# Three-stage attention and expert kernel on one core: border columns copied by the engines that make the parts, padding cleared ahead, low parts of the weights on VectorE, and the work between two stages laid out anew

## The chip, the core and the metric

One core of a Trainium2 chip. The metric is the device time of one execution in microseconds; three runs of the kernel before gave 1315.1 us in the median (1314.43 to 1315.68). The engines are named as in the profile: PE is TensorE's matmul, PEld its weight load, DVE VectorE, ACT ScalarE, POOL GpSimd, SP SyncE, which issues nearly all DMAs.

## What is computed

For 8 batches of 576 positions, 8 heads of 64:

```python
kv  = einsum('bhsd,bhse->bhde', k, v)
x   = einsum('bhsd,bhde->bhse', q, kv); x = x / sqrt(mean(x*x) + 1e-6) * g_norm   # 4608 x 512
h   = relu(x @ w_in)                                   # 512 -> 1024
y   = (h * sigmoid(conv3(h, conv_w))) @ w_out          # conv3: three taps along the positions, zero padding
out = y + relu(layernorm(y) * g_ln @ w_ch1) @ w_ch2    # 512 -> 2048 -> 512
```

## The kernel before

**Number format.** Each fp32 operand of the large products is a high part, rounded to TensorE's fp32r format by a copy, and a low part (value less high part); a product is three passes, high x high, high x low, low x high. High parts are copies on ACT, low parts subtractions on DVE or POOL. Three weight matrices arrive as 8-byte numbers and are first converted (`cv_act` on ACT, `cv_vec` on DVE, `cv_pool` on POOL, L245 to L269).

**Stage A**, the first 535 us. The 4608 positions are 36 tiles of 128 (t), three to a chunk (c = 0 to 11). A tile is made by `qkv` (PE), `st_a`, `st_v`, `st_p`, `x_norm` (ACT, DVE, POOL, DVE), `tx_first` (PE transpose), then `xe_a` (L479, ACT, high part) and `xe_l` (L502, DVE, low part) into the chunk's two tiles x_t[c]. These are 386 or 388 columns wide: 384 positions and border columns, which belong to the neighbouring chunk or are zero at the edges of a group of three chunks. `new_xt` (L457) allocates them and clears the zero columns on POOL; `xe_h` (L512) copies the border columns on POOL, two copies for each part, when the first tile of a chunk is there. So the first product of a chunk that is not the last of its group waits for the first tile of the next chunk and for `xe_h`. For each i (8 slices of 128 hidden columns in each of 12 chunks): `gemm1` (L534, 12 matmuls), `conv_a`, `conv_t`, `conv_v` (ACT, ACT, DVE twice, L582), `gate_a`, `gate_v` (ACT, DVE L599), `gsplit_a`, `gsplit_l` (ACT, DVE or POOL, L608), `gemm2` (L610, 9 matmuls). The last `gemm2` of a chunk is followed by `y_evac` and `y_store`.

**Stage B**, from 535 us. Six chunks of 768 positions. `ln_stat`, `ln_p`, `ln_a` normalise a tile (DVE L716 to L719, POOL, ACT); for chunk 0 it is turned by PE (`tz_first`, `tz_evac`), for the others by 16 stream transposes on DVE (`tz`, L750, through `blocks`, L470). The first product uses seven matrix products in place of eight: `z_sum` (L753, four DVE subtractions) and `z_hi`, `z_lo` (L766, L771) make seven factors. A chunk has 8 blocks (p). In a block PE runs p1, p2, p6, p5, p7, p4, p3 (L783, six matmuls each) and, between them, 12 `part`s of the block before (L861, three matmuls each). They share two PSUM banks for the first product: p1 of the next block waits until `r_lo` "21" (L843, DVE) has read the bank that p4 ended, p2 of the next until `c_add` "12" (L831, DVE) has read that of p3.

**Weights of stage B.** w_ch1 is split during stage A: `w1_sum`, `w1_hi` (ACT), `w1_lo` (L677, POOL, 32 subtractions: 24 of 128x512, 8 of 128x256), `w1_store` to DRAM. w_ch2 is converted and split (16 slices, `split_w1` on POOL, L289) during the blocks of chunk 0, two slices to a block, and stored for the later chunks.

**Order.** Every step has a slot, a number; the program is all steps in order of slot, and each engine takes its instructions in that order. `at(slot, fn, ...)` sets it; for slots before 25 two lists of names (`ORDERS`) replace it. gemm1 of slice i stands at slot 2i, its chain one to three slots later, its gemm2 at 2i + 7; so slot 160 is the first gemm1 of chunk 10. END_A = 192 is the slot of p1 of the first block, a block has 14 slots. Lines L981 to L1118 place the steps that the change moves. Buffers come from rotating pools; `xt` holds six tiles, for x_t, and later for z's inputs and sums.

Of the kernel before, what the change touches and what calls it, by code (L numbers as in the profile page):

```python
# [10 lines left out]
F32 = mybir.dt.float32  # L11
# [1162 lines left out]
```

## Time and profile before

| | |
|---|---|
| median of three runs | 1315.1 us (1314.43 to 1315.68) |
| the profiled execution | 1316.47 us |
| its span in the trace | 1314.7 us |
| busy in the span: PE, PEld, DVE | 1270.2, 1135.6, 902.5 us |
| ACT, POOL | 550.8, 277.7 us |
| mean granted clock of TensorE | 0.984 |

The profiled execution lies 1.4 us above the median; 1.8 us of it lie outside the span. A row of the timeline is a start, a duration, engine, line, operation, what it writes and reads, how many alike follow each other, and in brackets how long the engine was idle before and what ended that. A row of the windows gives the busy time of each engine in a stretch, TensorE's granted clock (1.00 is 2.4 GHz, 0.50 is 1.2 GHz), the busy share of the DMA engines and their GB/s.

### The profile page before, as it was taken

To read this page: it belongs to the slowest core of one execution; us is meant where nothing else is said; L and a number is where in the kernel's file an instruction comes from. 1 tells how busy PE (TensorE), PEld (TensorE's weight loads), DVE (VectorE), ACT (ScalarE), POOL (GpSimd) and SP (SyncE) were. 2 spreads that over 40 slices of the span, in tenths; PEclk is the share of its full clock that TensorE was granted. 3 is DMA by queue.
4 is the path that set the end of the run, shared out by engine and by line. 5 is a ranking of instruction groups with operands and counts; after the bars stand their busy time and mean duration, and the time that the engine had idled before them with its cause. 6 is when DMAs were issued, how large, how long until landed. Compare 5 with 4: busy or idle time off the path is not lost.

```text
span 1314.7 us, 19363 instructions
## 1 busy us (share of the span) xinstructions
PE 1270.2 (97%) x6949; PEld 1135.6 (86%) x6949; DVE 902.5 (69%) x1755; ACT 550.8 (42%) x1067; POOL 277.7 (21%) x296
## 2 busy tenths in 40 slices
PE   6789999999999999899999999999999999999998
PEld 5678898989888899788889898999999899998997
DVE  4898887878888877777766666667666766663223
ACT  3664565655665566544342223223322322232221
POOL 3473543332333321233310100000000001000000
PEclk9789999999999999999999999999999999999999
DMA  9455366345643223477668674865676576656561
GB/s 299 110 158 141 104 185 160 110 143 149 171 119 100 86 96 113 153 256 256 248 248 298 206 233 157 307 193 192 229 251 202 183 286 222 206 206 256 176 224 49
DMA packets 184052, 245.90 MB, mean 187 GB/s; under 512 B 92668, under 2 KB 121364, under 8 KB 183956
## 3 DMA queue, kind: packets, MB, share of 16 engines
q1 hardware_dynamic: 182032, 243.59, 57.6%
q10 hardware_dynamic: 1924, 1.07, 0.3%
q8 instruction: 55, 0.90, 0.3%
q14 instruction: 41, 0.34, 0.1%
HBM read 202.66 MB, written 41.94 MB: 186 GB/s over the span
## 4 chain that ended last, share of the span: by engine, by line
PE 60%; DVE 19%; ACT 8%; SPq 5%; DMA 4%; issue 3%; POOL 1%; DVEq 0%; ACTq 0%; POOLq 0%
PE accB L861 27%; PE u L783 14%; PE v L783 7%; DVE a L582 6%; PE c L783 4%; PE accA L617 4%; SPq L391 4%; PE h L542 3%; DVE a L599 2%; DVE zx L475 2%; ACT a L558 1%; ACT g L603 1%; ACT a L593 1%; DVE g L608 1%; ACT hs L567 1%
## 5 line engine op out<-in xcount | busy, mean ns | idle before, releaser
L861 PE MATMUL accB<-w2s,r 128*128 128x512 f32 x1440 | 376.1, 393 | 0.0
L861 PEld LDWEIGHTS accB<-w2s,r 128*128 128x128 f32 x1440 | 267.3, 188 | 38.5
L783 PE MATMUL u<-z,w1s 128*128 128x384 f32 x1152 | 235.4, 339 | 8.3 <-DVE r L843 5.7
L542 PE MATMUL h<-xt,win 128*128 128x386 f32 (+1 forms) x1152 | 226.6, 346 | 6.3 <-POOL xt L519 6.2
L783 PEld LDWEIGHTS u<-z,w1s 128*128 128x128 f32 x1152 | 207.0, 188 | 27.6 <-DVE r L843 8.6
L617 PE MATMUL accA<-wout,g 128*128 128x512 f32 x864 | 223.9, 404 | 2.2 <-DVE ya L627 1.2
L542 PEld LDWEIGHTS h<-xt,win 128*128 128x128 f32 x1152 | 206.4, 192 | 14.8 <-POOL xt L519 8.5
L617 PEld LDWEIGHTS accA<-wout,g 128*128 128x128 f32 x864 | 160.9, 191 | 34.4 <-DVE ya L627 2.1
L838 ACT ACTIVATE r<-t 128x384 fp32r<-128x384 f32 x144 | 75.7, 526 | 262.5 <-DVE t L831 262.5
L825 ACT COPY u<-u 128x384 f32<-128x384 f32 x144 | 68.7, 477 | 217.8 <-PE u L783 217.8
L582 DVE SCALAR_TENSOR_TENSOR a<-hs,cols,a 128x384 f32<-128x384 f32 x192 | 137.2, 714 | 29.5 <-ACT a L558 25.5
L475 DVE STREAM_TRANSPOSE zx<-xc 32x128 f32<-32x128 f32 x480 | 145.2, 303 | 7.5
L843 DVE SCALAR_TENSOR_TENSOR r<-t,r 128x384 fp32r<-128x384 f32 x144 | 80.4, 558 | 85.3 <-ACT r L838 85.3
L726 POOL TENSOR_SCALAR mv<-mv 128x1 f32<-128x1 f32 x36 | 25.0, 694 | 478.8 <-DVE mv L717 470.9
L783 PE MATMUL v<-z,w1s 128*128 128x384 f32 x576 | 116.9, 337 | 0.0
L783 PEld LDWEIGHTS v<-z,w1s 128*128 128x128 f32 x576 | 103.7, 188 | 8.2
L831 DVE TENSOR_TENSOR t<-v,u 128x384 f32<-128x384 f32 x96 | 53.4, 556 | 73.7 <-ACT u L825 55.4
L593 ACT ACTIVATE a<-a 128x384 f32<-128x384 f32 x96 | 50.4, 525 | 114.3 <-DVE a L582 114.2
L447 POOL TENSOR_TENSOR r<-ss,mhalf 128x8 f32<-128x8 f32 x36 | 66.8, 1856 | 77.5 <-DVE ss L442 75.2
L861 PE MATMUL accB<-w,r 128*128 128x512 f32 x288 | 77.7, 402 | 0.0
L268 POOL TENSOR_TENSOR cvw<-cvw,rnw 128x512 int32<-128x512 int32 x32 | 43.3, 1353 | 160.5 <-DVE cvw L261 108.2
L599 DVE TENSOR_TENSOR a<-hs,a 128x384 f32<-128x384 f32 x96 | 62.9, 655 | 19.1 <-ACT a L593 18.9
(106 smaller groups left out, 1380.3 us busy)
## 6 DMA issues: line engine op xcount, KB each, us to landing
w1s<-w_d SPq DMA_DIRECT2D x144, 512.0 KB, 5.5
w2s<-w_d SPq DMA_DIRECT2D x80, 512.0 KB, 5.2
raw_w<-in_moe_w_ch SPq DMA_DIRECT2D x32, 512.0 KB, 5.6
w_d<-w1f SPq DMA_DIRECT2D x24, 512.0 KB, 2.8
w1s<-w_d SPq DMA_DIRECT2D x48, 256.0 KB, 5.4
y_dr<-ya SPq DMA_DIRECT2D x36, 256.0 KB, 2.3
yb<-y_dr SPq DMA_DIRECT2D x36, 256.0 KB, 5.4
yr<-y_dr SPq DMA_DIRECT2D x36, 256.0 KB, 6.1
```

Source lines behind the costliest of these rows:

```text
L447: nc.gpsimd.tensor_tensor(out=r, in0=x_r[t], in1=mhalf, op=ALU.pow)
L475: nc.vector.transpose(out=out[32 * i : 32 * i + 32, :, a : a + 32], in_=src[a : a + 32, :, i, :])
L542: nc.tensor.matmul(ps[:, 0:n], lhsT=w[:, a, kk, :], rhs=x_t[c][b][:, kk, 0:n], start=(m == 0), stop=(m == 3 * KD - 1),)
L582: nc.vector.scalar_tensor_tensor(out=av, in0=segs(c, h, j), scalar=cols[:, j * FA + f : j * FA + f + 1], in1=av, op0=ALU.mult, op1=ALU.add,)
L593: nc.scalar.activation(out=a, in_=a, func=ACTF.Sigmoid)
L599: nc.vector.tensor_tensor(out=av, in0=segs(c, h, 1), in1=av, op=ALU.mult)
L617: nc.tensor.matmul(acc[c][r], lhsT=g[:, a, r * P : (r + 1) * P], rhs=w[:, b, :], start=(f == 0 and n == 0), stop=(f == FA - 1 and n == len ...
L783: nc.tensor.matmul(ps[:, 0:HT], lhsT=w[:, a, kk, :], rhs=z[b][:, kk, :], start=(start and n == 0), stop=(n == 5), skip_group_check=True,)
L825: nc.scalar.copy(out=t, in_=ch[c, p, "u"][:, 0:HT])
L838: nc.scalar.activation(out=g[:, HI, :], in_=cu[c, p, h], func=ACTF.Relu)
L843: engine.scalar_tensor_tensor(out=g[:, LO, :], in0=cu.pop((c, p, h)), scalar=0.0, in1=g[:, HI, :].bitcast(F32), op0=ALU.max, op1=ALU.subtract)
L861: nc.tensor.matmul(ch[c][r], lhsT=g[:, a, rr * P : (rr + 1) * P], rhs=w[:, b, :], start=(p == 0 and n < RB and m == 0), stop=(p == NPB - 1 ...
```

## The change

1. **Border columns.** `xe_h` is gone. `border` copies the columns of the high part on ACT at the end of `xe_a`, those of the low part on DVE at the end of `xe_l`.
2. **Padding.** `new_xt` is a step of its own: chunks 0 to 2 at the very start, the others some slots ahead of their first `xe_a` (chunk 11 just ahead).
3. **w_ch1's low parts** (`w1_lo`) move from POOL to DVE, in the same slots.
4. **w_ch2's conversion and split** get new slots within the block, and `split_w1` moves from POOL to DVE.
5. **Chunk 0 of stage B**: `ln_stat` and what follows move from slots 160 to 180 to slots 148 to 168, `z_sum` from 186 to 178 and 180.4 (two halves), `z_hi` and `z_lo` from 187 to 194 to 179 to 193.
6. **Later chunks of stage B**: `z_sum` in two halves, the transposes `tz` in two halves of 8, other slots for the seven factors.
7. **End of stage A**: the last `gemm2` is issued tile by tile between p7, p4, p3 and p1, with one `y_evac` behind each.
8. `kv_pair` of batches 3 to 7: the four steps follow each other; the two lists for slots before 25 have a new order (only a few lines are shown).

```diff
--- before.py
+++ after.py
@@ ORDERS, second list
...
-        round_w0_win3 xe_h_3 xe_h_0 xe_h_1 gemm1_0 load_q2_3 cv_vec_win3 round_w0_win4 round_w0_wout0 consts3 conv_a_0
-        cv_pool_win3 consts4 load_w_wout7 kv_pair_1_0 kv_pair_1_1 cv_vec_win4 cv_pool_win4 load_w_wout4 load_w_wout5 consts5
...
+        round_w0_win3 load_q2_3 cv_vec_win3 round_w0_win4 round_w0_wout0 gemm1_0 conv_a_0 cv_pool_win3 consts3
+        consts4 cv_vec_win4 consts5 cv_pool_win4 kv_pair_1_0 load_w_wout4 kv_pair_1_1 load_w_wout7 kv_pair_1_2 load_w_wout5
...
@@ -454,6 +454,7 @@
             in1=x_r.pop(t).rearrange("p (h o) -> p h o", o=1).to_broadcast([P, H, D]),
             op=ALU.mult,
         )
+
     def new_xt(c):
         x_t[c] = [xt_p.tile([P, KD, XW], F32R, tag="xt", name=f"xt{c}_{a}") for a in range(2)]
         o, n = ((0, 1), (CH // 2 + 1, 2), (CH + 1, 1))[c % 3]
@@ -467,19 +468,26 @@
             nc.tensor.transpose(ps[:, j * P : (j + 1) * P], src[:, j * P : (j + 1) * P], ident)
         tp_ps[t] = ps.rearrange("p (k s) -> p k s", k=KD)
 
-    def blocks(out, src):
+    def blocks(out, src, rows=range(0, P, 32)):
 
         src = src.rearrange("p (k i j) -> p k i j", k=KD, i=P // 32)
-        for a in range(0, P, 32):
+        for a in rows:
             for i in range(P // 32):
                 nc.vector.transpose(out=out[32 * i : 32 * i + 32, :, a : a + 32], in_=src[a : a + 32, :, i, :])
 
     xe = {}
 
+    def border(t, a, copy):
+
+        c, r = divmod(t, TPC)
+        if r == 0 and c % 3 != 0:
+            here, prev = x_t[c][a], x_t[c - 1][a]
+            last = CH + 3 if (c - 1) % 3 == 1 else CH + 1
+            copy(out=prev[:, :, last : last + 1], in_=here[:, :, 1:2].bitcast(F32))
+            copy(out=here[:, :, 0:1], in_=prev[:, :, last - 1 : last].bitcast(F32))
+
     def xe_a(t):
         c, r = divmod(t, TPC)
-        if r == 0:
-            new_xt(c)
         xt = x_t[c]
         xf = tp_ps.pop(t)
         half = CH // 2
@@ -497,6 +505,7 @@
         for o, n, col in pieces:
             hi = xt[HI][:, :, col : col + n]
             nc.scalar.copy(out=hi, in_=xf[:, :, o : o + n])
+        border(t, HI, nc.scalar.copy)
         xe[t] = pieces, xf
 
     def xe_l(t, engine):
@@ -508,16 +517,7 @@
             engine.tensor_tensor(
                 out=xt[LO][:, :, col : col + n], in0=xf[:, :, o : o + n], in1=hi.bitcast(F32), op=ALU.subtract
             )
-
-    def xe_h(t):
-        c, r = divmod(t, TPC)
-        xt = x_t[c]
-        if r == 0 and c % 3 != 0:
-            prev = x_t[c - 1]
-            last = CH + 3 if (c - 1) % 3 == 1 else CH + 1
-            for a in range(2):
-                nc.gpsimd.tensor_copy(out=prev[a][:, :, last : last + 1], in_=xt[a][:, :, 1:2].bitcast(F32))
-                nc.gpsimd.tensor_copy(out=xt[a][:, :, 0:1], in_=prev[a][:, :, last - 1 : last].bitcast(F32))
+        border(t, LO, engine.tensor_copy)
 
 
     h_ps = {}
@@ -607,12 +607,12 @@
         a, g = a_sb.pop(i), g_sb[i]
         engine.tensor_tensor(out=g[:, LO, :], in0=a, in1=g[:, HI, :].bitcast(F32), op=ALU.subtract)
 
-    def gemm2(c, f):
+    def gemm2(c, f, tiles=range(TPC)):
         if f == 0:
             acc[c] = [ps_acc.tile([P, 512], F32, tag="acc", name=f"accA{c}_{r}") for r in range(TPC)]
-        g = g_sb.pop(c * FA + f)
+        g = g_sb[c * FA + f]
         w = wt["wout", f]
-        for r in range(TPC):
+        for r in tiles:
             for n, (a, b) in enumerate(PASSES):
                 nc.tensor.matmul(
                     acc[c][r],
@@ -650,6 +650,7 @@
     z_p = {}
     z_t = {}
     z_f = {}
+    z_more = {}
     w_f = {}
     w_t = {}
     ch = {}
@@ -747,8 +748,12 @@
     def tz_evac(c, r):
         nc.scalar.copy(out=new_z(c, r), in_=z_p.pop((c, r)))
 
-    def tz(c, r):
-        blocks(new_z(c, r), xc.pop((c, r)))
+    z_part = {}
+
+    def tz(c, r, i):
+        if i == 0:
+            z_part[c, r] = new_z(c, r), xc.pop((c, r))
+        blocks(*z_part[c, r], range(64 * i, 64 * i + 64, 32))
 
     def z_sum(c):
 
@@ -759,9 +764,16 @@
         sub = nc.vector.tensor_tensor
         sub(out=t12[:, 0], in0=b12, in1=b11, op=ALU.subtract)
         sub(out=t12[:, 1], in0=b22, in1=t12[:, 0], op=ALU.subtract)
-        sub(out=t34[:, 0], in0=b22, in1=b12, op=ALU.subtract)
-        sub(out=t34[:, 1], in0=b21, in1=t12[:, 1], op=ALU.subtract)
         z_t[c] = [b11, b21, t12[:, 1], t12[:, 0], t34[:, 0], b22, t34[:, 1]]
+
+        def rest():
+            sub(out=t34[:, 0], in0=b22, in1=b12, op=ALU.subtract)
+            sub(out=t34[:, 1], in0=b21, in1=t12[:, 1], op=ALU.subtract)
+
+        z_more[c] = rest
+
+    def z_sum2(c):
+        z_more.pop(c)()
 
     def z_hi(c, m):
         z = [big.tile([P, 2, HT], F32R, tag="big", name=f"z{c}_{m}_{a}") for a in range(2)]
@@ -971,8 +983,9 @@
     def h_xe(t):
         head(xe_a, t)
         head(xe_l, t, nc.vector)
-        head(xe_h, t)
-
+
+    for c in range(3):
+        at(START - 0.97, new_xt, c)
     h_q(0)
     h_q(1)
     head(x_norm, 0)
@@ -999,8 +1012,8 @@
 
     for c in range(NC):
         for r in range(TPC):
-            at(SA * c + SA - 2 + LAG + (1 if c < NC - 1 else 5), y_evac, c, r, nc.vector if r == 1 else nc.scalar)
-        at(SA * c + SA - 2 + LAG + (2 if c < NC - 1 else 6), y_store, c)
+            at(SA * c + SA - 2 + LAG + (1 if c < NC - 1 else 5.5 + 2 * r), y_evac, c, r, nc.vector if r == 1 else nc.scalar)
+        at(SA * c + SA - 2 + LAG + (2 if c < NC - 1 else 9.6), y_store, c)
     for t in range(len(HEAD), NT):
         s = tau(t)
         _, o_st, o_nm, _, o_xe = steps(t)
@@ -1008,9 +1021,10 @@
         for fn in (st_a, st_v, st_p):
             at(s + o_st, fn, t)
         at(s + o_nm, x_norm, t)
+        if t >= 3 * TPC and t % TPC == 0:
+            at(s + (o_st if t // TPC < NC - 1 else o_xe), new_xt, t // TPC)
         at(s + o_xe, xe_a, t)
         at(s + o_xe, xe_l, t, nc.vector)
-        at(s + o_xe, xe_h, t)
     for b in range(1, B):
         at(tau(kv_tile[b]) - 1, kv_evac, b)
 
@@ -1049,14 +1063,22 @@
         at(s + 4, w1_sum, p)
         for j in range(4):
             at(s + 5 + 2 * j, w1_hi, p, j)
-            at(s + 5 + 2 * j, w1_lo, p, j, nc.gpsimd)
+            at(s + 5 + 2 * j, w1_lo, p, j, nc.vector)
             at(s + 6 + 2 * j, w1_store, p, j)
     for f in range(FB):
-        s = END_A - 4 + 7 * f
-        at(s - 5, load_w, ("w2", f), src_out(w2, f))
-        rnd(s, ("w2", f))
-        spl(s + 3, ("w2", f), nc.gpsimd)
-        at(s + 4, w2_store, f)
+        p, i = divmod(f, 2)
+        s = END_A + SP * p
+        key = ("w2", f)
+        at(s - 9 + 6 * i, load_w, key, src_out(w2, f))
+        for fn, o in (
+            (round_w0, (-2, 3)[i]),
+            (cv_vec, (2.8, 10.7)[i]),
+            (cv_pool, (2.9, 10.8)[i]),
+            (split_w0, (8.6, 12.6)[i]),
+        ):
+            at(s + o, fn, key)
+        at(s + (10.65, 13)[i], split_w1, key, nc.vector)
+        at(s + (11, 14)[i], w2_store, f)
 
     for c in range(CB):
         for p in range(NPB):
@@ -1067,7 +1089,7 @@
                     at(s + 0.2, w2_load, c, 2 * p + i)
         for r in range(RB):
             if c == 0:
-                s = 160 + 4 * r
+                s = 148 + 4 * r
                 at(s - 6, y_load, c, r, "b")
                 at(s, ln_stat, c, r)
                 at(s, ln_p, c, r)
@@ -1080,11 +1102,14 @@
                 at(s, ln_stat, c, r)
                 at(s, ln_p, c, r)
                 at(s + 3, ln_a, c, r)
-                at(s + 4, tz, c, r)
-        at(END_A - 6 if c == 0 else base(c - 1, 7) - 3, z_sum, c)
+                at(s + 4, tz, c, r, 0)
+                at(s + 12.65, tz, c, r, 1)
+        s = END_A - 14 if c == 0 else base(c - 1, 7) + 0.9
+        at(s, z_sum, c)
+        at(s + (2.4 if c == 0 else 12.4), z_sum2, c)
         order = (M_A11, M_A12, M_S2, M_S1, M_S3, M_A22, M_S4)
         for n, m in enumerate(order):
-            s = END_A + (-5, -4, -3, -2, -1, 1, 2)[n] if c == 0 else base(c - 1, 7) + 2 * n + 1
+            s = END_A + (-13, -11, -9, -7, -5, -2, 1)[n] if c == 0 else base(c - 1, 7) + (1, 3, 5, 8, 14.9, 17.3, 19.3)[n]
             at(s + 0.1, z_hi, c, m)
             at(s + 0.2, z_lo, c, m, nc.vector)
         for r in range(RB):
@@ -1122,10 +1147,14 @@
         c, f = divmod(i, FA)
         at(2 * i, gemm1, i)
         s = 2 * i + LAG
-        at(s if s < END_A else END_A + 2 * (s - END_A) - 1, gemm2, c, f)
+        if i < FA * NC - 1:
+            at(s if s < END_A else END_A + 2 * (s - END_A) - 1, gemm2, c, f)
+        else:
+            for r in range(TPC):
+                at(END_A + 9 + 2 * r, gemm2, c, f, (r,))
     for b in range(1, B):
         for j in range(NP):
-            at(tau(kv_tile[b]) - 5 + j, kv_pair, b, j)
+            at(tau(kv_tile[b]) - (3 if b > 2 else 5 - j), kv_pair, b, j)
     for t in range(len(HEAD), NT):
         s = tau(t)
         at(s + steps(t)[0], qkv, t)
```

## Rows read from the trace of the kernel before

**Rows 1.** The page, first two lines: span, and what TensorE (PE) was busy.
```profile
span 1314.7 us, 19363 instructions
...
PE 1270.2 (97%) x6949; PEld 1135.6 (86%) x6949; DVE 902.5 (69%) x1755; ACT 550.8 (42%) x1067; POOL 277.7 (21%) x296
```

**Rows 2.** Windows: us of busy time by engine and (instructions), PEclk, DMA share, GB/s.
```profile
0.00:100.00 100.00, 74.57 (x512) 66.54 (x513) 73.34 (x121) 55.81 (x106) 55.02 (x60) 0.86 0.70 187
100.00:427.00 327.00, 324.37 (x2128) 288.02 (x2127) 264.88 (x450) 187.28 (x374) 117.87 (x118) 1.00 0.50 139
427.00:460.00 33.00, 31.42 (x166) 28.01 (x164) 28.09 (x48) 19.63 (x40) 11.38 (x11) 1.00 0.24 86
460.00:535.00 75.00, 74.40 (x382) 67.75 (x383) 58.98 (x101) 46.72 (x91) 13.91 (x18) 0.98 0.26 92
535.00:670.00 135.00, 124.43 (x584) 108.27 (x584) 100.48 (x214) 62.64 (x120) 46.18 (x43) 0.96 0.67 237
670.00:1314.70 644.70, 641.05 (x3183) 576.98 (x3181) 376.69 (x825) 178.68 (x340) 33.32 (x49) 1.00 0.64 217
```

**Rows 3.** Timeline, TensorE, 320 to 680 us: matmuls after an idle time, in brackets.
```profile
337.41 2.20 PE L542 MATMUL h<-xt,win 128*128 128x388 f32 x11 [0.36 <-POOL xt L519]
...
459.14 0.45 PE L542 MATMUL h<-xt,win 128*128 128x388 f32 x1 [1.16 <-POOL xt L519]
...
460.60 3.55 PE L542 MATMUL h<-xt,win 128*128 128x388 f32 x11 [1.02 <-POOL xt L519]
...
540.73 1.33 PE L783 MATMUL u<-z,w1s 128*128 128x384 f32 x6 [2.52 <-ACT u L825]
...
554.96 1.66 PE L783 MATMUL u<-z,w1s 128*128 128x384 f32 x6 [2.53 <-DVE r L843]
...
572.91 1.32 PE L783 MATMUL u<-z,w1s 128*128 128x384 f32 x6 [0.43 <-DVE r L843]
...
589.97 1.31 PE L783 MATMUL u<-z,w1s 128*128 128x384 f32 x6 [1.10 <-DVE r L843]
...
660.35 1.31 PE L783 MATMUL c<-z,w1s 128*128 128x384 f32 x6 [2.29 <-DVE t L831]
```

**Rows 4.** Windows of 10 us around two of these (columns as in rows 2).
```profile
459.00:469.00 10.00, 8.84 (x42) 8.14 (x43) 8.17 (x16) 5.28 (x11) 3.99 (x8) 0.83 0.47 162
...
587.00:597.00 10.00, 8.90 (x44) 7.61 (x43) 6.37 (x12) 5.64 (x11) 3.68 (x4) 1.00 0.50 165
```

**Rows 5.** Timeline, TensorE: the same nine matmuls behind a long idle time and later.
```profile
541.90 3.81 PE L617 MATMUL accA<-wout,g 128*128 128x512 f32 x9
...
547.96 2.25 PE L617 MATMUL accA<-wout,g 128*128 128x512 f32 x9
```

**Rows 6.** Timeline, VectorE (DVE) and GpSimd (POOL), 453 to 460 us.
```profile
450.08 1.65 DVE L599 TENSOR_TENSOR a<-hs,a 128x384 f32<-128x384 f32 x1
...
457.35 1.27 POOL L679 TENSOR_TENSOR w1f<-ws,w1f 128x512 fp32r<-128x512 f32 x1
...
457.51 2.18 DVE L582 SCALAR_TENSOR_TENSOR a<-hs,cols,a 128x384 f32<-128x384 f32 x2 [0.48 <-ACT a L558]
...
459.61 0.69 DVE L508 TENSOR_TENSOR xt<-tx,xt 128x512 fp32r<-128x512 f32 x1
```

**Rows 7.** Groups by line, VectorE: count, busy us, mean ns, idle time before.
```profile
L716 DVE BATCH_NORM_STATS2 st<-yb 128x6 f32<-128x512 f32 x36 | 24.7, 686 | 0.0
...
L451 DVE TENSOR_TENSOR xn<-x,r 128x512 f32<-128x512 f32 x36 | 24.5, 682 | 4.3 <-POOL r L447 4.1
...
L719 DVE SCALAR_TENSOR_TENSOR xc<-yb,mv,gb 128x512 f32<-128x512 f32 x36 | 28.8, 801 | 1.5
...
L717 DVE BATCH_NORM_AGGREGATE mv<-st 128x2 f32<-128x6 f32 x36 | 6.6, 182 | 2.8
```

**Rows 8.** Timeline, VectorE, 655 us: the first of four subtractions for the next chunk.
```profile
655.23 1.86 DVE L760 TENSOR_TENSOR t<-zx,zx 128x768 f32<-128x768 f32 x1
```

**Rows 9.** Window of one block of the last stage (columns as in rows 2).
```profile
570.00:586.35 16.35, 15.92 (x80) 14.02 (x79) 12.56 (x30) 7.21 (x14) 6.26 (x6) 1.00 0.72 251
```

More of the change, by code (lines that the diff above doesn't have):

```diff
@@ new lines @@
+        conv_t_0 conv_v_0 gate_a_0 cv_vec_wout0 gemm1_1 conv_a_1 kv_pair_1_3 gate_v_0 cv_pool_wout0 split_win0_3
+        split_w0_wout0 split_win1_3 conv_t_1 conv_v_1 split_win0_4 split_win1_4 round_w0_wout1 gsplit_a_0 kv_evac_1
+        gsplit_l_0 gate_a_1 gate_v_1 load_w_wout6 round_w0_win5 gemm1_2 cv_vec_wout1 cv_vec_win5 cv_pool_wout1
+        split_w0_wout1 split_w1_wout0 tq_blocks_4 cv_pool_win5 tq_blocks_5 load_kvh_2_0 conv_a_2 conv_t_2 gsplit_a_1
+        gsplit_l_1 split_w1_wout1 load_kvh_2_1 conv_v_2 round_w0_wout2 cv_vec_wout2 cv_pool_wout2 gate_a_2 gate_v_2 gemm1_3
@@ new lines @@
+        qkv_4 split_win0_5 st_a_4 st_v_4 qkv_5 round_w0_win6 st_a_5 st_p_4 split_win1_5 cv_vec_win6 cv_pool_win6
+        split_w0_wout2 split_w1_wout2 x_norm_4 conv_a_3 conv_t_3 conv_v_3 st_v_5 round_w0_win7 gsplit_a_2 gsplit_l_2 gemm1_4
+        tx_first_4 round_w0_wout3 st_p_5 gate_a_3 cv_vec_win7 split_win0_6 split_win1_6 cv_vec_wout3 cv_pool_wout3 conv_a_4
+        gemm1_5 conv_a_5 conv_t_4 gate_v_3 xe_a_4 split_w0_wout3 split_w1_wout3 tq_blocks_6 round_w0_wout4 x_norm_5 conv_v_4
+        gsplit_a_3 gemm2_0_0 qkv_6 gate_a_4 load_q2_5 st_a_6 gemm2_0_1 gemm2_0_2 xe_l_4 cv_vec_wout4 conv_t_5 gsplit_l_3
@@ new lines @@
+        tq_blocks_7 cv_pool_win7 split_win0_7 cv_pool_wout4 load_q2_4 st_v_6 gemm1_6 split_w0_wout4 tx_first_5 gate_v_4
+        gsplit_a_4 split_w1_wout4 round_w0_wout5 conv_v_5 st_p_6 x_norm_6 split_win1_7 gsplit_l_4 gate_a_5 xe_a_5 load_kvr_2
+        round_w0_wout6 cv_vec_wout5 xe_l_5 gemm1_7 cv_vec_wout6 gate_v_5 cv_pool_wout5 split_w0_wout5
+        tx_first_6 xe_a_6 conv_a_6 conv_t_6 xe_l_6 cv_pool_wout6 split_w0_wout6 conv_v_6 split_w1_wout5 gemm2_0_3 gemm2_0_4
+        gsplit_a_5 gate_a_6 gate_v_6 qkv_7 st_a_7 st_v_7 conv_a_7 round_w0_wout7 gemm1_8 gsplit_l_5 conv_t_7 conv_v_7
@@ new lines @@
+        gate_a_7 st_p_7 gemm1_9 x_norm_7 conv_a_8 gsplit_a_6 gate_v_7 tx_first_7 xe_a_7 gsplit_a_7 load_kvh_3_0 gsplit_l_7
+        split_w1_wout6 tq_blocks_8 gsplit_l_6 conv_a_9 conv_t_8 cv_vec_wout7 load_kvh_3_1 load_kvr_3 gemm1_10 conv_v_8
+        gate_a_8 xe_l_7 gemm2_0_5 gemm2_0_6 conv_t_9 gate_v_8 gsplit_a_8 conv_v_9 cv_pool_wout7 qkv_8 st_a_8 gemm1_11
+        split_w0_wout7 conv_a_10 st_v_8 split_w1_wout7 gemm2_0_7 gate_a_9 gate_v_9 gsplit_l_8 tq_blocks_9 kv_pair_2_0
+        st_p_8 x_norm_8 kv_pair_2_1 kv_pair_2_2 kv_pair_2_3 conv_t_10 gsplit_a_9 y_evac_0_0 y_evac_0_1 y_evac_0_2 conv_v_10
@@ L98 @@
+        gate_a_10 tx_first_8 xe_a_8 kv_evac_2 gate_v_10 conv_a_11 conv_t_11 gsplit_l_9 gemm2_1_0 qkv_9 xe_l_8 conv_v_11
         gate_a_11 gate_v_11 gsplit_a_10 gsplit_l_10 tq_blocks_10 gsplit_a_11 gsplit_l_11 load_w_w10 gemm1_12 conv_a_12
-        conv_t_12 conv_v_12 gemm2_1_1 xe_h_8 load_q2_6 y_store_0
+        conv_t_12 conv_v_12 load_q2_6 gemm2_1_1 y_store_0
 """),
```

48 lines of the change are left out of this document (14 added, 34 removed).

## The prediction

> **What bounds the kernel now.** I read the page first: PE is busy 1270.2 of 1314.7 us [rows 1]. So a change that adds no matmul and takes none away, as this one, can win at most the 44.5 us in which PE stands still and what PE loses at the lower clock. The windows tell where they lie [rows 2]. In the first 100 us PE is idle for 25.4 us, from 100 to 427 for 2.6, from 427 to 535 for 2.2, from 535 to 670 for 10.6; behind 670 it is idle for 3.7 us, nearly all of it the tail. The last stage, half of the span, can win nothing. What is within reach is the passage from stage A to stage B, and the last chunks before it.
>
> The timeline of TensorE names the waits there [rows 3]. PE waits at slot 160 (459 us) for the border copies, at 540.7 for ACT's copy of u, at 555.0 and then once a block for `r_lo` on VectorE, at 660.4 for `c_add` on VectorE. Each is a wait for an engine that takes its steps in order and has something less urgent ahead. A second price hangs on the long ones: in the 10 us from the border wait on, the granted clock is 0.83 in the mean, while the wait of 1.10 us at 590 leaves it at 1.00 [rows 3, 4]. The drop to 0.50, the 1.2 GHz level, is priced by nine matmuls of one kind, 3.81 us right behind a wait and 2.25 us later [rows 5]: 1.56 us. The stretches 427 to 460 and 460 to 535 show what VectorE has to spare: it is busy 28.1 of 33 us and 59.0 of 75 [rows 2].
>
> **The change part by part, against the profiled execution (1316.47 us).**
>
> *Wait at 540.7.* p6 waits for u, whose copy stands on ACT behind the sigmoid of the last slice, and that behind `conv_v` on VectorE. Before, VectorE has z_sum and five z_lo in slots 186 to 192; the change leaves two z_lo there and moves the conversion of the first w_ch2 slice behind the urgent steps. Between gemm1 of the last slice and p6, PE has two gemm2 and two products of its own, which hides the chain once the queue ahead is gone. Now: 2.52 idle + 1.56 slow = 4.1 us. I leave 0.3: **3.8 won**.
>
> *Wait at 555.0.* p1 of the second block waits for `r_lo` "21". Ahead of it stand two `y_evac`, a conversion on ACT and the same conversion on VectorE. The change puts the conversion and `split_w1` behind `r_lo` "21", and issues the last gemm2 in three parts, so that one `y_evac` stands there, not two. It costs 2.53 + 1.56 = 4.1; **3.8 won**.
>
> *Waits once a block.* Five of 0.41 to 0.43 us (the first is shown) and one of 1.10 [rows 3], 3.2 us. They go if VectorE keeps up, and here the change gives it more to do. A block takes 16.35 us with VectorE busy for 12.56 [rows 9]; two `split_w1` come from POOL, 128x512 with two inputs, which is a `x_norm` in size: 0.68 us [rows 7]. That is 13.9 of the 15.9 us that a block keeps without its wait, PE's busy time in it [rows 9]. It fits with 2.0 us to spare, but in order: `split_w1` of the second slice now waits on VectorE for ACT's high part, behind a half `tz` and `r_lo` "12", right before the part that needs it; queued behind it are `ln_stat` and the next `c_add` "11", for which p5 waits. On SP the store of that slice waits for it too, with the loads of the block after next behind it, which have most of a block. I leave 0.8 us over all blocks: **2.4 won**.
>
> *Wait at 660.4.* Four subtractions stand ahead of `c_add` "12"; the first took 1.86 us [rows 8]. Now two go behind it, to the start of the next block, and two stand ahead of the `c_add` "12" of that block; of the seven z_lo that stood in that block, four are left. It costs 2.29 + 1.56 = 3.9. Two subtractions can still hold up a `c_add`, so I leave 1.0 of idle time, which the wait at 590 shows to be too short for the clock: **2.9 won**.
>
> *Slot 160, the border columns.* Now 1.16 + 1.02 idle + 1.56 slow = 3.7 us [rows 3]. The handover gains little: ACT writes the high part's border at once, but the low part's product still waits for `xe_l` on VectorE, at 459.61 [rows 6], and two small copies behind it (about 0.2 us each, by the smallest VectorE row [rows 7], where POOL's way from the end of `xe_l` to the product took 460.60 - 460.30 = 0.3 [rows 3, 6]). What decides is when VectorE gets there. By slot 160 it has three `ln_stat` more, 0.69 + 0.18 + 0.80 = 1.7 us each [rows 7], 5.0 in all, and two `w1_lo`, 1.4. It is spared what POOL's w1_lo cost it: while one ran, a pair of `conv_v` took 2.18 us, without one 1.27 [rows 6]; 0.9 each, 1.8 in all. Of its 4.9 us of idle time in this stretch I take half as filled, since they are waits for ACT's link of the chain, in which the new work fits. 5.0 + 1.4 - 1.8 - 2.5 = 2.1 us later. PE then waits from 457.98 to about 462.7, less one matmul: 4.3 + 1.56 = 5.9; two groups of transposes that move ahead on PE make it a little less, and I take 5.7. **2 lost.** The ends: nothing of the wait is left (3.7 won), and none of the spared time and none of the idle time is had (4.3 us more, 6 lost with another drop).
>
> *The rest of stage A.* 32 `w1_lo` on VectorE cost 24 x 0.68 and eight of half the size, some 20 us, and spare up to 32 x 0.9 = 29 where a two-input step ran beside each; VectorE is busy 81% from 100 to 427 [rows 2]. PE waits there in one place for the border, 0.36 us [rows 3]: **0.3 won**. The padding steps run on POOL ahead of use; only chunk 11's finds the pool `xt` full, with an input of stage B in it already, and waits, as `xe_l` does, for gemm1 of slot 158, which is done when PE begins to wait at 457.98. `kv_pair` moves within PE's order and adds nothing. The first 100 us have a new order, the same work and the same loads in nearly the same order on SP, whose transfers end the waits there: 0, with 3 us to each side.
>
> Sum: 3.8 + 3.8 + 2.4 + 2.9 - 2.0 + 0.3 = 11.2. 1316.5 - 11.2 = 1305.3, and 1304 beside the median, which lies 1.4 lower.
>
> **The rivals.**
>
> *VectorE becomes the bound (slower).* Place: the starts of chunks 7, 9 and 10 and the blocks of the first chunk. It decides once VectorE's delay at the first tile of a chunk exceeds what PE still has to do. At 337 that is so by 0.36 us already, so any work more there shows. If four w1_lo, 2.7 us, come late by the start of such a chunk and nothing is spared, PE waits 2.3 us at two more starts with a drop each (2 x 3.9 = 7.8), slot 160 loses 6, and the waits once a block and at 660 stay: 3.8 + 3.8 - 7.8 - 6 = 6.2 slower, 1321. For it: VectorE is busy for 28.1 of the 33 us before slot 160 [rows 2]. Against: the 0.9 us that each POOL step takes from VectorE now. Chance 0.10. The Trainium skill speaks for this rival: "Perfetto Trace Analysis", section "Optimizing Scalar/DVE Operations", says that with a saturated VectorE one should move work off it, to ScalarE or even GpSimd, and this change moves 48 subtractions the other way. The same passage adds that GpSimd shares a port with VectorE, so that moving work between these two might not help; by its first half the time would be this rival's, and it is the second that the trace bears out, 2.18 us beside a POOL step against 1.27 [rows 6].
>
> *The passage wins less.* VectorE is so full in the blocks of chunk 0 that `split_w1` of the second slice comes late: the waits once a block and at 660 stay as they are, in other places. 3.8 + 3.8 - 2 = 5.6 won, or 2.6 with 3 us lost in the first 100 us: 1309.5 to 1312.5. Chance 0.18.
>
> *All waits go, at slot 160 too.* 4.1 + 4.1 + 3.2 + 3.9 + 3.7 + 0.4 = 19.4: 1296. For it: POOL's steps beside VectorE cost it more than w1_lo costs. Chance 0.14.
>
> *It doesn't do what it says*: buffers or SP's queue hold the earlier steps where they were (a z tile waits for a weight's buffer), and the time stays at 1315. Chance 0.05.
>
> **How the numbers follow.** The forecast, 1298 to 1309, has 0.53. A measurement of this kernel can tell about 0.2%, 2.6 us, from no change. Faster by more: the forecast, the case of all waits and two thirds of the one that wins less, 0.79; the same: the rest of it and the last rival, 0.11; slower: 0.10. The range from 1296 to 1314 leaves out the slow rival and the last one.
>
> **What would show it.** Right: no wait over 1 us between 535 and 670, and a granted clock of 1.00 there; a block of about 15.9 us with VectorE busy near 14; one wait of 3 to 5 us at the first gemm1 of chunk 10, ended by a copy on VectorE. Wrong: waits for VectorE at other chunk starts, p5 or a part waiting for VectorE in each block, or a first stage that ends later than before by more than 3 us.

## The result and the profile after

The changed kernel takes 1296.53 us in the median (four runs, 1294.62 to 1297.92), the kernel before beside it 1315.39 (1314.43 to 1315.81). The ratio is 0.9853 with a 95% interval of 0.9838 to 0.9867: 19 us faster. Forecast were 1304 and a range of 1296 to 1314, so the direction holds and the time lies at the low end. It is also the price of the rival in which all waits go (1296), but that is luck: they did not all go, and a third of the gain came from where that rival had 0.4 us. The profiled execution of the changed kernel is its fastest (1294.62).

The page, then the windows of the changed kernel (columns and stretches as in [rows 2]):

```profile
span 1292.8 us, 19282 instructions
...
PE 1256.4 (97%) x6949; PEld 1130.5 (87%) x6949; DVE 905.0 (70%) x1819; ACT 554.7 (43%) x1083; POOL 210.3 (16%) x216
```

```profile
0.00:100.00 100.00, 72.37 (x505) 64.84 (x506) 72.09 (x123) 56.85 (x110) 48.77 (x50) 0.85 0.71 187
100.00:427.00 327.00, 325.89 (x2165) 294.69 (x2164) 271.81 (x501) 192.81 (x392) 83.90 (x72) 1.00 0.52 144
427.00:460.00 33.00, 31.12 (x174) 27.92 (x173) 30.56 (x57) 21.75 (x44) 10.38 (x12) 1.00 0.25 90
460.00:535.00 75.00, 74.18 (x376) 66.45 (x375) 56.27 (x95) 47.51 (x92) 6.26 (x7) 1.00 0.29 102
535.00:670.00 135.00, 133.68 (x664) 119.39 (x662) 111.08 (x241) 64.15 (x123) 28.72 (x28) 1.00 0.73 259
```

From 535 to 670 PE's idle time fell from 10.6 us to 1.3 and the granted clock rose from 0.96 to 1.00, as forecast. But from 100 to 427, where only 2.6 us of idle time could be seen before, PE now does 37 matmuls more in the same 327 us, and PEld is busy for 6.7 us more. Most of that gain stood in no idle column.

TensorE's timeline, the waits of 0.5 us or more behind 100 us:

```profile
274.94 0.97 PE L617 MATMUL accA<-wout,g 128*128 128x512 f32 x3 [1.11 <-DVE ya L627]
...
455.12 2.19 PE L542 MATMUL h<-xt,win 128*128 128x388 f32 x11 [1.85 <-DVE xt L486]
...
531.70 1.33 PE L795 MATMUL u<-z,w1s 128*128 128x384 f32 x6 [0.66 <-ACT u L837]
...
536.71 1.31 PE L795 MATMUL u<-z,w1s 128*128 128x384 f32 x6 [0.53 <-ACT u L837]
...
646.57 1.31 PE L795 MATMUL u<-z,w1s 128*128 128x384 f32 x6 [0.79 <-ACT u L837]
```

Where the time was won is read best from start times: the first matmul of a chunk or a block in either trace. Each difference is the changed kernel's start less that of the kernel before, and the last column is what the stretch from the line above brought. The two profiled executions lie 21.9 us apart, 3 more than the medians. The wait at 555.0 of the kernel before ends where block 1 begins, so it counts, like the one at 540.7, in the line of block 1.

| first matmul of | before | after | difference | won since the line above |
|---|---|---|---|---|
| chunk 2 | 131.71 | 132.98 | +1.27 | -1.3 |
| chunk 9 | 419.87 | 414.10 | -5.77 | 7.0 |
| chunk 11 | 498.75 | 492.78 | -5.98 | 0.2 |
| block 0 | 533.75 | 526.67 | -7.07 | 1.1 |
| block 1 | 554.96 | 542.27 | -12.69 | 5.6 |
| block 2 | 572.91 | 558.08 | -14.82 | 2.1 |
| block 7 | 655.38 | 636.49 | -18.89 | 4.1 |
| block 8 | 675.24 | 653.28 | -21.96 | 3.1 |

Behind block 8 the difference stays at 21.8 to 21.9 to the end.

### The profile page after: what moved, and what is told of

Read it like the earlier page. It is cut to its first block, busy times and chain, and to the rows that moved or that the text cites. A ratio compares the mean times of both kernels' runs of the same rounds, so it can differ in the third digit from the quotient of the medians.

```text
span 1292.8 us, 19282 instructions
## 1 busy us (share of the span) xinstructions
PE 1256.4 (97%) x6949; PEld 1130.5 (87%) x6949; DVE 905.0 (70%) x1819; ACT 554.7 (43%) x1083; POOL 210.3 (16%) x216
## 4 chain that ended last, share of the span: by engine, by line
PE 75%; DVE 10%; ACT 5%; SPq 4%; DMA 4%; issue 2%; DVEq 0%; ACTq 0%
PE accB L873 30%; PE u L795 15%; PE accA L617 8%; PE v L795 8%; PE h L542 7%; PE c L795 4%; SPq L391 3%; DVE a L582 3%; DVE a L599 1%; DMA kvr<-in_v 1%; PE x L424 1%; ACT a L558 1%; ACT g L603 1%; DMA vm<-in_v 1%; PE kv L359 1%
## 5 line engine op out<-in xcount | busy, mean ns | idle before, releaser
L617 PE MATMUL accA<-wout,g 128*128 128x512 f32 x864 | 220.5, 399 | 1.3 <-DVE ya L627 1.1
L542 PEld LDWEIGHTS h<-xt,win 128*128 128x128 f32 x1152 | 205.9, 191 | 15.7 <-issue 6.8
L582 DVE SCALAR_TENSOR_TENSOR a<-hs,cols,a 128x384 f32<-128x384 f32 x192 | 125.1, 651 | 30.3 <-ACT a L558 26.6
L603 ACT CAST g<-a 128x384 fp32r<-128x384 f32 x96 | 49.1, 512 | 65.3 <-DVE a L599 63.7
```

What stands on the lines that cost most here:

```text
L542: nc.tensor.matmul(ps[:, 0:n], lhsT=w[:, a, kk, :], rhs=x_t[c][b][:, kk, 0:n], start=(m == 0), stop=(m == 3 * KD - 1),)
L582: nc.vector.scalar_tensor_tensor(out=av, in0=segs(c, h, j), scalar=cols[:, j * FA + f : j * FA + f + 1], in1=av, op0=ALU.mult, op1=ALU.add,)
L603: nc.scalar.copy(out=g[:, HI, :], in_=a_sb[i])
L617: nc.tensor.matmul(acc[c][r], lhsT=g[:, a, r * P : (r + 1) * P], rhs=w[:, b, :], start=(f == 0 and n == 0), stop=(f == FA - 1 and n == len ...
```

## The experiments

The "difference" is that of a run's ratio (to the kernel before, on the same chip) and 0.9853, times 1315.4 us. An interval of a ratio is about 1.9 us to each side, that of a difference about 2.7. The first row of this table is a change of the kernel before and stands against that.

| run | median us | ratio, interval | difference |
|---|---|---|---|
| kernel before, kv_pair grouped | 1315.51 | 0.9998, 0.999 to 1.0007 | -0.3 |
| kv_pair spread | 1300.46 | 0.9884, 0.987 to 0.9897 | +4.1 |
| w1_lo on POOL | 1306.99 | 0.9931, 0.9914 to 0.9948 | +10.3 |
| both of these | 1307.72 | 0.994, 0.9927 to 0.9954 | +11.4 |
| border on POOL | 1294.72 | 0.9843, 0.9829 to 0.9856 | -1.3 |
| w_ch2 in its old slots | 1308.14 | 0.9938, 0.9924 to 0.9952 | +11.2 |
| w_ch2's split on POOL | 1296.95 | 0.9853, 0.9839 to 0.9866 | 0.0 |
| chunk 0's z late | 1297.29 | 0.9855, 0.9842 to 0.9869 | +0.3 |
| tz whole | 1305.51 | 0.9925, 0.9913 to 0.9938 | +9.5 |
| tz whole, z_sum in its old slots | 1307.44 | 0.9941, 0.9928 to 0.9955 | +11.6 |
| lists of before | 1294.19 | 0.984, 0.9826 to 0.9853 | -1.7 |
| a combination | 1294.48 | 0.9841, 0.9827 to 0.9854 | -1.6 |

**kv_pair: spread again, and grouped alone.**

```diff
-            at(tau(kv_tile[b]) - (3 if b > 2 else 5 - j), kv_pair, b, j)
+            at(tau(kv_tile[b]) - 5 + j, kv_pair, b, j)
```

> The changed kernel with one part undone: the four kv_pair steps of batches 3 to 7 stand again between other matmuls, one slot apart, as before. Theory (switch): every change of TensorE from a group of 128-column matmuls to the 64-column matmuls of kv_pair and back costs some 0.25 us, ten entries and ten exits before against five and five in the changed kernel; the gaps at these places shrank by 3.8 us in sum, so this gives 1296.5 + 3.8 = 1300.3, and the start of chunk 9 comes 3.8 us later. Rival (VectorE relieved): the 7.0 us that stage A won come from w1_lo having left POOL, and the gaps at kv_pair only moved; then this stays within 0.5 us of the changed kernel, 1296 to 1297.

> The kernel before with one part of the change alone: the four kv_pair steps of batches 3 to 7 follow each other directly. Theory (switch): 3.8 us less, 1311.6 against 1315.4. Rival (VectorE relieved): 1315.4, within 0.5 us.

Undone in the changed kernel it costs 4.1 us; done alone in the kernel before it brings nothing. The switch theory is right in size (though it counted ten entries before, and there are 20), and incomplete. TensorE's timeline of the changed kernel, then of this run, around one batch:

```profile
217.00 0.69 PE L359 MATMUL kv<-vm,kl 128*64 128x64 f32 x16
217.51 0.29 PE L359 MATMUL kv<-kvr 128*64 128x64 f32 x4
217.63 0.64 PE L359 MATMUL kv<-vm,kl 128*64 128x64 f32 x16
```

```profile
215.57 0.69 PE L359 MATMUL kv<-vm,kl 128*64 128x64 f32 x16
216.09 0.29 PE L359 MATMUL kv<-kvr 128*64 128x64 f32 x4
216.31 2.41 PE L542 MATMUL h<-xt,win 128*128 128x388 f32 x12
218.64 0.69 PE L359 MATMUL kv<-vm,kl 128*64 128x64 f32 x16
```

No row has an idle time in brackets. The cost shows in the starts (0.22 us from the last short group to `h`, 0.12 to another kv group) and on PEld, by groups of lines from 131 to 419 us, first the changed kernel, then this run:

```profile
L359 PEld LDWEIGHTS kv<-vm,kl 128*64 128x64 f32 x320 | 11.0, 138 | 1.5 <-issue 1.5
```

```profile
L359 PEld LDWEIGHTS kv<-vm,kl 128*64 128x64 f32 x320 | 10.9, 137 | 6.2 <-issue 6.2
```

Fifteen entries more (20 instead of 5) at 4.1 us are some 0.27 us each, an estimate. The page cannot show this as idle: from 131 to 250 us PE counts as busy for 119.00 of 119.00 us in both kernels, with 781 matmuls in the changed one and 769 in this.

Why it brings nothing alone is in TensorE's timeline of the kernel before with kv_pair grouped:

```profile
335.11 0.45 PE L542 MATMUL h<-xt,win 128*128 128x388 f32 x1 [1.69 <-POOL xt L519]
335.92 3.67 PE L542 MATMUL h<-xt,win 128*128 128x388 f32 x11 [0.36 <-POOL xt L519]
```

PE arrives earlier and waits for the border: where one wait of 0.36 us stood [rows 3], there are 2.05 us and a stretch at the lower clock. The wait at slot 160 and those in the passage behind it are as before.

**w1_lo on POOL again, and both undone.**

```diff
-            at(s + 5 + 2 * j, w1_lo, p, j, nc.vector)
+            at(s + 5 + 2 * j, w1_lo, p, j, nc.gpsimd)
```

> The changed kernel with w1_lo back on POOL, all else as changed. Theory (switch for 3.8 us, w1_lo for the other 3): the small waits for y_evac at 153 to 155 (0.9 to 1.0 us each before) and the border wait at 337 (0.36) come back, the two-input VectorE steps beside POOL's are longer again (L582 at 714 ns in the mean against 651, L599 at 655 against 593), and chunk 10 waits about as long as now since the two w1_lo that leave VectorE there are made up by the slower steps: 2 to 4 us more, 1298.5 to 1300.5. Rival (VectorE relieved explains all of stage A): 6 to 7 us more, 1303. Second rival, the one that the prediction feared (work on VectorE delays chunk 10): the wait of 1.85 us at 455 shrinks and the time falls by 1 to 2 us, 1295.

> The changed kernel with kv_pair spread as before and w1_lo on POOL as before, both at once, all else as changed. Theory (the two need each other: what TensorE saves at kv_pair is only time in which it then waits for VectorE, unless VectorE is relieved too): no more than w1_lo on POOL alone cost, 10.5, so 1306 to 1308. Rival (two separate gains, 3.9 and 10.5): 1311.

10.3 us, more than either theory gave; and with kv_pair spread as well 11.4, which is 1.1 more and not 4.1. Between these two numbers the errors leave some room; the start times, and the run of kv_pair alone, say the same. From the start of chunk 2 to that of chunk 9 the changed kernel takes 281.1 us, 285.4 with kv_pair spread, 286.8 with w1_lo on POOL and 287.8 with both; the kernel before 288.2, and 287.1 with kv_pair grouped. So the two parts together account for this stretch, and they need each other, as the theory of that run had it: while w1_lo is on POOL, VectorE's chain sets the pace and time saved on TensorE is waited out (with w1_lo alone on POOL TensorE waits 1.47 + 1.03 us at chunk 7, with kv_pair spread too only 0.80). TensorE's timeline with w1_lo on POOL:

```profile
336.98 0.41 PE L542 MATMUL h<-xt,win 128*128 128x388 f32 x1 [1.47 <-ACT xt L487]
338.42 3.71 PE L542 MATMUL h<-xt,win 128*128 128x388 f32 x11 [1.03 <-DVE xt L487]
...
422.46 2.19 PE L542 MATMUL h<-xt,win 128*128 128x386 f32 x11 [0.83 <-DVE xt L487]
...
462.69 0.42 PE L542 MATMUL h<-xt,win 128*128 128x388 f32 x1 [0.64 <-ACT xt L487]
...
465.61 3.90 PE L542 MATMUL h<-xt,win 128*128 128x388 f32 x11 [2.50 <-DVE xt L486]
```

The work of chunks 2 to 8 is the same in both kernels, so their stretches can be compared: first the changed kernel, then this run (columns as in [rows 2]).

```profile
132.98:414.10 281.12, 280.01 (x1854) 253.50 (x1852) 233.09 (x432) 169.01 (x344) 69.93 (x60) 1.00 0.51 141
```

```profile
134.52:421.30 286.78, 282.63 (x1854) 255.11 (x1852) 233.15 (x400) 168.54 (x343) 103.07 (x87) 0.99 0.49 136
```

VectorE is busy for 233.1 us in both, though in the changed kernel 27 w1_lo stand on it in this stretch. The same window for w1_lo's line alone, in the changed kernel, has them at 17.8 us; so on POOL they took about as much from VectorE's other steps. (The stretches are not quite equal: the changed kernel's has five other short steps more, 2.5 us. Line by line, steps of equal number are 16.7 us longer with w1_lo on POOL.)

```profile
132.98:414.10 281.12, 17.77 (x27) 1.00 0.51 141
```

Groups of lines from 131 to 427 us show where: first VectorE in the changed kernel, then in this run.

```profile
L582 DVE SCALAR_TENSOR_TENSOR a<-hs,cols,a 128x384 f32<-128x384 f32 x118 | 76.2, 646 | 20.6 <-ACT a L558 18.5
L599 DVE TENSOR_TENSOR a<-hs,a 128x384 f32<-128x384 f32 x60 | 35.1, 586 | 9.5 <-ACT a L593 9.4
```

```profile
L582 DVE SCALAR_TENSOR_TENSOR a<-hs,cols,a 128x384 f32<-128x384 f32 x115 | 83.9, 729 | 20.1 <-ACT a L558 17.9
L599 DVE TENSOR_TENSOR a<-hs,a 128x384 f32<-128x384 f32 x57 | 37.9, 664 | 10.7 <-ACT a L593 10.6
```

The work is about equal, its place is not. On POOL, w1_lo lengthens `conv_v` (L582) and the gate (L599), links of the chain that each wait for ACT and for which ACT waits; on VectorE it stands by itself in the queue and is waited for by none of them. Steps that read only one tile from SBUF kept their length (`x_norm` L451, 684 and 683 ns). And it is not that POOL's own steps come late: from 131 to 510 us of this run neither TensorE nor VectorE nor ACT waits for POOL anywhere. One case, in the timelines of VectorE and POOL with w1_lo on POOL:

```profile
461.84 1.63 DVE L608 TENSOR_TENSOR g<-a,g 128x384 fp32r<-128x384 f32 x1
...
461.71 1.34 POOL L680 TENSOR_TENSOR w1f<-ws,w1f 128x512 fp32r<-128x512 f32 x1
```

`gsplit_l` (L608), 0.55 us without a POOL step beside it (the same step at 452.44 of the changed kernel), takes 1.63 and ends 0.4 us behind POOL's step. The Trainium skill, "SBUF — State Buffer", section "SBUF: two separate sides", says that a VectorE instruction with two SBUF inputs and a GpSimd one that reads SBUF hold one pair of ports by turns, each for its whole duration. This row agrees: 1.08 us of POOL's 1.34 were added.

**The border on POOL.** Both copies on POOL behind the low part, those on ACT and VectorE left out.

```diff
-        border(t, HI, nc.scalar.copy)
...
-        border(t, LO, engine.tensor_copy)
+        border(t, HI, nc.gpsimd.tensor_copy)
+        border(t, LO, nc.gpsimd.tensor_copy)
```

> The changed kernel with the border columns copied on POOL again, both parts behind the low part, all else as changed. Theory: the copies cost a handover and POOL's own time, 0.3 us and four copies of 0.3 at each chunk start that has no slack: the wait at chunk 10 grows from 1.85 by about 1 us and the one at 337 comes back, 1 to 2.5 us more with at most one clock drop, 1297.5 to 1299. Rival (the border copies are what the change gained at slot 160): 3.5 us or more, 1300 and above. If POOL, now free of w1_lo, takes them at once, 0.

The difference is -1.3, within its error. The wait at chunk 10 is 0.22 + 0.96 us in this run and 1.85 in the changed kernel, both ended by a border copy. So the handover itself won nothing that can be measured: with w1_lo off POOL, POOL's copies come in time.

**w_ch2 in its old slots, and its split on POOL.** The first run takes back the block of slots as it stood before, POOL's `split_w1` included; the second only the engine:

```diff
-        at(s + (10.65, 13)[i], split_w1, key, nc.vector)
+        at(s + (10.65, 13)[i], split_w1, key, nc.gpsimd)
```

> The changed kernel with w_ch2's conversion and split in the slots of before and its split_w1 on POOL, all else as changed. Theory (the order on VectorE and ACT made the waits once a block): the wait at the start of the second block (2.53 us and a drop of 1.56 before) comes back at least in part, and five to seven waits of 0.4 to 1.1 us once a block: 3 to 7 us more, 1299.5 to 1303.5. Rival (these waits went with the last gemm2's three parts and z_lo's new slots): within 1 us of the changed kernel, 1295.5 to 1297.5.

> The changed kernel with the 16 split_w1 of w_ch2 back on POOL, in the new slots. Theory (slots decide, not the engine): a block of 15.7 us has VectorE busy for some 14; taking 1.36 off it and slowing its two-input steps beside POOL's 1.3 us each leave it below 15, TensorE stays the bound: within 1 us, 1295.5 to 1297.5. Rival (as w1_lo on POOL cost 10.5 us in stage A, a POOL step beside VectorE's costs here too): the waits once a block come back, 0.4 to 1 us in each of 7 blocks, 3 to 7 us more, 1299.5 to 1303.5.

The old slots cost 11.2 us, the old engine nothing. TensorE's timeline with the old slots:

```profile
541.71 1.32 PE L795 MATMUL u<-z,w1s 128*128 128x384 f32 x6 [1.27 <-ACT u L837]
...
545.65 1.32 PE L795 MATMUL u<-z,w1s 128*128 128x384 f32 x6 [0.17 <-DVE r L855]
...
564.25 1.33 PE L795 MATMUL u<-z,w1s 128*128 128x384 f32 x6 [2.67 <-DVE r L855]
```

These are not the two waits of the kernel before. The second block begins at 545.65, and where 2.53 us were waited for `r_lo` "21" [rows 3] it waits 0.17, although the conversion stands ahead of `r_hi` and `r_lo` again (the last gemm2 is in three parts, as in the changed kernel). The wait of 1.27 us is at p4, for the third copy of u, not at p6. The one of 2.67 is a block later, and ACT's timeline names its start: the conversion ahead of `r_hi` waits for the weight's transfer.

```profile
561.26 0.66 ACT L253 ACTIVATE cvw<-raw_w 128x512 f32<-128x512 f32 x1 [3.57 <-DMA raw_w<-in_moe_w_ch]
```

The kernel before has no such wait: there ACT waits for a transfer of w_ch2 for 0.6 us in all from 510 to 680, and this slice is loaded 5.8 us into its block, here 8.2. So part of the 11.2 us, 2.8 from block 1 to block 2 by the starts, comes of old slots in a new surrounding. The waits once a block are back in part: 2.2 us from block 2 to block 7, of the 4.1 won.

**Chunk 0's z late.** `ln_stat`, z_sum, z_hi and z_lo of chunk 0 take the slots of before (160 + 4r, END_A - 6, END_A - 5 to + 2).

> The changed kernel with chunk 0 of stage B (ln_stat, z_sum, z_hi, z_lo) in the slots of before, all else as changed. Theory: the wait for u some 15 us into stage B comes back (2.5 us and a drop, 4.1) while the wait of 1.85 us at chunk 10 goes, as three ln_stat of 1.62 us stand behind it again: 2 to 4 us more, 1298.5 to 1300.5. Rival (VectorE, freed of POOL's steps, catches up by itself): the wait at u does not come back and the one at chunk 10 goes: 1 to 2 us less, 1295.

The theory is wrong about u and the rival about the time, which is unchanged. The waits at u are 0.79 and 0.72 us (0.66 and 0.53 in the changed kernel), with no drop. Chunk 10 starts without its wait, which by the starts wins 3.2 us up to chunk 11; 2.3 of these are lost again up to block 1.

**tz and z_sum.** First both halves of tz in one place; then, besides, z_sum in one piece at base - 3 and the factors at base + 1 to base + 13.

```diff
-                at(s + 12.65, tz, c, r, 1)
+                at(s + 4, tz, c, r, 1)
```

> The changed kernel with both halves of tz in one place, the slot of before, and z_sum, z_hi and z_lo in their new slots. Theory (16 transposes in a row stand ahead of c_add in each of six blocks): the wait of 0.85 us for c_add, 1.35 us a block with what follows, is all back, but the one of 3.18 us at the last block is not: 6 x 1.35 = 8 more, 1304.6. Rival (z_sum and z_lo in their old slots made the 10.9 us of that run, by a later start of each block): 1297, within 1 us.

> The changed kernel with z_sum, both halves of tz, z_hi and z_lo of the later chunks in the slots of before, all else as changed. Theory: the wait for c_add at the last block of the first chunk comes back, 2.3 us and a drop of 1.56: 3.9 us more, 1300.4, and no later chunk shows it, as in the kernel before. Rival (the four subtractions were slow, 1.86 us the first, because POOL's split_w1 ran beside them): they take some 1.2 us each, the wait shrinks to about 1 us without a drop: 1 us more, 1297.5.

tz alone is 9.5 us. VectorE's timeline, then TensorE's, with tz whole:

```profile
554.71 5.04 DVE L476 STREAM_TRANSPOSE zx<-xc 32x128 f32<-32x128 f32 x16
559.79 0.56 DVE L843 TENSOR_TENSOR t<-v,u 128x384 f32<-128x384 f32 x1
```

```profile
560.40 1.32 PE L795 MATMUL v<-z,w1s 128*128 128x384 f32 x6 [0.86 <-DVE t L843]
...
577.45 1.31 PE L795 MATMUL v<-z,w1s 128*128 128x384 f32 x6 [0.85 <-DVE t L843]
```

Sixteen transposes stand ahead of `c_add`, in six blocks, which take 17.0 us each. In the kernel before, with whole tz too, such a block takes 16.35 [rows 9]: what tz costs here it costs together with the other steps that moved into the block, and no run takes these apart. The old slots of z_sum add 2.1 us to that, within the error, and one wait, at the last block of the first chunk, of 3.18 us (2.29 in [rows 3]):

```profile
652.22 2.29 PE L795 MATMUL c<-z,w1s 128*128 128x384 f32 x6 [3.18 <-DVE t L843]
```

The expectation of that run put the whole of its cost on z_sum and was wrong by 7 us: it left out that the run also made tz whole.

**The lists of before, and a combination.** The first run takes the old order of the slots before 25. The second takes the old order, the border on POOL and `ln_stat` one step later (152 + 4r).

> The changed kernel with the two lists for the slots before 25 in the order of before (without the names of the step that is gone), all else as changed. Theory (the new order costs the head): chunk 2 starts at 134.5 us in the mean of eight traces with the new lists (132.98 to 135.65) and at 131.9 in two with the old ones (131.71 and 132.10), so 2.6 us less, 1294. Rival (the first 100 us scatter with the loads, whatever the order): 1296.5, within 1 us.

> A version meant to beat the changed kernel: the lists of before for the slots before 25, the border copies on POOL behind the low part, and ln_stat of chunk 0 of stage B one step later (slots 152 to 172). Theory (three separate gains): 2.6 for the lists, 1.8 for the border (measured), 1 for one ln_stat less ahead of chunk 10: 1291. Rival (what one gains the next wait takes): 1294 to 1295, as with the border on POOL alone.

With the old lists chunk 2 starts at 130.99 us, with the new ones at 132.98; over all traces here it is 132.98 to 136.73 in ten with the new lists and 130.99 to 133.18 in four with the old. So the new order costs the first 100 us some 2 to 3. In the time it is -1.7, within the error. The combination gives no more than either alone: its rival was right. Neither is shown to beat the changed kernel.

## Why the prediction was right, and where it was wrong

The forecast was right in direction, and in range only just: 1296.5 lies 0.5 us from its low end. Its sum of 11.2 us came out at 18.9 between the medians and 21.9 between the two profiled executions, from which the terms below are read. The terms of the passage held within 2 us; the rest of stage A was mis-sized by 6.7 and slot 160 by 3.3. That the range reached down this far was owed to a rival with another mechanism. Of its signs, three came (no wait over 0.8 us between 535 and 670, a granted clock of 1.00, blocks of 15.7 us); the wait at chunk 10 was 1.85 us in place of 3 to 5.

- *The bound.* The first step said that the change can win at most the time in which PE stands still and what it loses at the lower clock. That is wrong: from chunk 2 to chunk 9 the same matmuls were counted busy for 285.8 us before and 280.0 after, at a clock of 1.00 in both. The kernel before (the changed kernel's window is above):

```profile
131.71:419.87 288.16, 285.78 (x1853) 253.71 (x1852) 233.30 (x395) 168.48 (x335) 106.64 (x105) 1.00 0.49 137
```

- *Waits at 540.7 and 555.0, 3.8 won at each*: 7.7 for both from block 0 to block 2, of which 0.4 is a wait once a block. At 540.7, 2.52 us and a drop became 0.66 and 0.53 without one. Why is open in part: with z_sum and z_lo in their old slots p6 waits 0.79, with the conversion in its old slots 0.76, so neither reason alone brings the wait back. The step left out POOL: the `conv_v` ahead of the copy took 2.24 us beside POOL's `split_w1` before and 1.27 in the changed kernel (VectorE's timelines below, before and after). But with the old slots it takes 2.26 again, and p6 waits only those 0.76; which of the three together make the wait was not tried.

```profile
537.52 2.24 DVE L582 SCALAR_TENSOR_TENSOR a<-hs,cols,a 128x384 f32<-128x384 f32 x2 [0.22 <-ACT a L558]
```

```profile
529.44 1.27 DVE L582 SCALAR_TENSOR_TENSOR a<-hs,cols,a 128x384 f32<-128x384 f32 x2
```

- *Of these the wait at 555.0* is gone, and stays away (0.17) with the conversion ahead of `r_lo` again. What is left of the step's reasons is the last gemm2 in three parts: between the starts of p4 and p1 TensorE now has 3.6 us of work, where it had 2.35 and the wait, and one `y_evac` is ahead on ACT, not two. That part was not undone by itself.
- *Waits once a block, 2.4 won*: 4.1 from block 2 to block 7 (2.8 of it idle time). The waits are all gone, and a block takes 15.67 us with VectorE busy for 13.37 (15.9 and 13.9 forecast). Moving `split_w1` was priced at 1.36 us a block, and the run shows it free. The working did not say that a whole tz would then cost 9.5 us: the halves are what keeps this gain.

```profile
558.08:573.75 15.67, 15.67 (x79) 14.13 (x78) 13.37 (x33) 7.96 (x16) 3.92 (x5) 1.00 0.78 292
```

- *Wait at 660.4, 2.9 won*: 3.1, for the reason given: with z_sum back in its old slots the wait is back, 3.18 us.
- *Slot 160, 2 lost*: 0.2 won up to chunk 11, 1.3 up to block 0 (13 matmuls moved from the second of these stretches into the first). The one wait of 3 to 5 us was forecast, and 1.85 came, without a drop of the clock. The working counted the 5.0 us of `ln_stat` right and took half of VectorE's idle time as filled, and POOL's cost from this stretch alone (1.8). With w1_lo on POOL the forecast wait comes: 0.64 + 2.50 us and a drop. (Of the 2.18 and 1.27 us by which POOL's cost was priced, [rows 6] shows the first only; the 1.27 there is POOL's step. A pair of `conv_v` without POOL does take 1.27, at 349.33 for one.)
- *The rest of stage A, 0.3 won*: 7.0, the failed term. It followed from the bound and was sized by the idle time in brackets (one wait of 0.36). Two things stand there that no bracket shows: 4.1 us of switching at kv_pair, costed at nothing ("adds nothing"), and VectorE's chain, lengthened by POOL, which had to be relieved for it to count. The working named 29 us as the most that could be spared on VectorE and 20 as added; in the stretch measured, what was spared (16.7) about equals the 17.8 that were added, and it still decided.
- *First 100 us, 0 with 3 to each side*: 1.3 lost, some 2 to 3 by the runs with the old lists.
- *The slow rival* failed: behind 100 us TensorE waits for VectorE over 0.5 us in two places only, 1.11 and 1.85. Its reason, that work moves onto a saturated VectorE, is answered by VectorE's 233.1 us with w1_lo on either engine.

The parts undone one by one cost 4.1 + 10.3 + 11.2 + 11.6 = 37 us, twice the 19 that were won: each keeps what the others gain, and an old slot among new ones can cost what it did not cost before (the weight's transfer above).

## What to carry to other kernels

A stretch in which TensorE counts as busy all the time can still hold time: compare the starts of equal work, and TensorE's weight loads, between two versions, and keep matmul groups of another shape together. Where two engines run nearly level, a saving on one shows only once the other is relieved, so test such parts in pairs. An element-wise step with two inputs on GpSimd is not free for VectorE, though it can be for the time where TensorE sets the pace (w_ch2's split: 0.0); in a queue in program order, long runs of small steps (16 transposes, 5 us) belong in halves behind the step that TensorE waits for.

## What the runs showed of the hardware that was not expected

Moving 27 subtractions, 17.8 us on VectorE, from POOL to VectorE left its busy time from chunk 2 to chunk 9 at 233.1 us.

The clock behind a wait is no fixed price. Behind a wait of 1.83 to 1.85 us at chunk 10 the same eleven matmuls took 2.19 us in the changed kernel and 3.46 with w_ch2's split on POOL; behind 2.50 us with w1_lo on POOL they took 3.90, and behind 2.51 with both parts undone 2.17. The granted clock over them was 1.00, 0.58, 0.50 and 1.00. The 1.56 us that the prediction put behind each long wait came out anywhere from 0 to 1.7.
